# Attention with relative bias, then a max-out feed-forward: scoring the left-over queries plainly at the head of the second visit, with both AV halves in the first

## The chip, the cores and the metric

One core of one Trainium2 chip. The metric is the time of one execution on the device, in microseconds, the median of several runs. Where two kernels are compared, the ratio is the mean time of one kernel's fast runs over that of the other's fast runs of the same rounds, so it is not quite the ratio of the medians that are quoted. With one core, a run is called slow when it is over 1.5% above the fastest run of the same kernel.

In the profile lines PE is TensorE, DVE VectorE, ACT ScalarE, POOL GpSimd and SP SyncE. A line of a timeline gives the start and the length in microseconds, engine, program line, operation, what is written `<-` what is read, the shape, and how many instructions are merged (`x8`); in brackets stands the idle time of the engine just before, and what ended it. The *span* is the time from the first to the last instruction of the profiled run.

## The reference

Eight batches of eight heads, 576 positions, head size 64. Attention with a bias that depends only on the distance of query and key; its output, 4608 rows of 512, goes through a max-out layer.

```python
scores = (1/8) * q @ k.T + bias_table[bucket(|i - j|)]     # 576 x 576 per head
attn   = exp(scores - max) / sum
x      = (attn @ v), heads side by side                    # 4608 x 512
h      = maximum(maximum(x @ w1, x @ w2), x @ w3)          # 4608 x 768
out    = h @ w_out                                         # 4608 x 512
```

576 is 4 x 128 + 64. So each head has four full tiles of 128 positions and 64 left-over ones, and two heads share one set of 128 rows ("a head pair", `hp`). The bias becomes a factor exp(bias), which differs from 1 only in a band around the diagonal and is multiplied in on VectorE ("the band product").

## The kernel before

TensorE, ScalarE (exp and some copies) and VectorE (band products, quotients, maxima, copies) work on two things at a time: the attention of one head pair, and the feed-forward of the batch before, handed out in portions. A pair has two halves. Each half begins with a *visit* (scores of 256 queries against 512 keys for both heads, in two buffers of two banks), then comes one half of the *previous* pair's AV (`next_late`), then a portion of the feed-forward (`fill`), with the scores of the left-over keys (first half) or left-over queries (second half) put in between. Names are shortened here and cuts are marked.

```python
ps_s: 2 buffers of 2 PSUM banks   # scores "sc", left-over keys "sct", left-over queries "scq"
ps_a: 2 buffers of 1 bank         # AV, "a"
ps_f: 2 buffers of 1 bank         # feed-forward, "ff"

def first(fb):  ps0 = bank(); product(ps0, fb, 0); ACT: m0 = copy(ps0)         # f
def second(fb): ps1 = bank(); product(ps1, fb, 1); DVE: m  = max(ps1, m0)      # m
def third(fb):  ps2 = bank(); product(ps2, fb, 2); DVE: hT = max(ps2, m)       # g
# a portion of an ordinary half: g of block fb-1, then f and m of block fb

def left_queries(hp, qT, kT, el):          # q tail is block diagonal: 128 columns for two heads
    sc = ps_s.tile([P, KT, 2 * 64], ...)
    for t in range(KT):
        mm(sc[:, t, :], lhsT=kT[:, P * t : P * t + P], rhs=qT[:, QM : QM + P])
    exp(eq, sc)

# second half of a pair
visit(qT, kT, e4, 1)                                   # 8 matmuls, two exps
quotients = next_late()                                # AV of the previous pair, half 1
times_band(hp, e4, 1, 0, QM, inorder)                  # band product
quotients()                                            # reciprocal, product into x_sb
...
def queries():
    left_queries(hp, qT, kT, el)
    times_band(hp, e4, 3, 0, QM, inorder)
fill(rate, lambda: times_band(hp, e4, 2, 0, QM, inorder), queries)
times_band_left(hp, el)
```

TensorE's and VectorE's instructions are kept in program order. With two "ff" banks, the third product of a portion (m) takes the bank of the first (g), which is free when VectorE has done g's maximum, hT.

The softmax here doesn't subtract the row's maximum and nothing guards it: scores larger than these inputs give would overflow.

## Time and profile before

| | before |
|---|---|
| time, median of 4 runs | 325.96 us (323.77 to 326.36) |
| span of the profiled run | 324.3 us |
| one batch in the steady part (first score matmul to that of the next batch) | 33.88 us |
| one pair with an ordinary portion in both halves | 8.47 us |
| PE idle before the feed-forward matmuls | 0.0 us |
| PE wait for keys transposed by DMA (batches 2 to 7) | none |

The batch time is read off the timeline of TensorE: the first score matmul of corresponding visits stands at 164.43 and 198.31 us. The lines themselves are in the prediction.

### The profile page before, as it was taken

To read this page: it belongs to the slowest core of one execution; us is meant where nothing else is said; L and a number is where in the kernel's file an instruction comes from. 1 tells how busy PE (TensorE), PEld (TensorE's weight loads), DVE (VectorE), ACT (ScalarE), POOL (GpSimd) and SP (SyncE) were. 2 spreads that over 40 slices of the span, in tenths; PEclk is the share of its full clock that TensorE was granted. 3 is DMA by queue.
4 is the path that set the end of the run, shared out by engine and by line. 5 is a ranking of instruction groups with operands and counts; after the bars stand their busy time and mean duration, and the time that the engine had idled before them with its cause. 6 is when DMAs were issued, how large, how long until landed. Compare 5 with 4: busy or idle time off the path is not lost.

```text
span 324.3 us, 8019 instructions
## 1 busy us (share of the span) xinstructions
PE 310.4 (96%) x3232; PEld 177.1 (55%) x3232; DVE 216.0 (67%) x537; ACT 201.8 (62%) x274; POOL 112.6 (35%) x151
## 2 busy tenths in 40 slices
PE   7757999999999999999999999999999999999995
PEld 2345776787555555555555555555555554444442
DVE  6476787777666766676667766777767675454452
ACT  3947798798677667776777677667776651121221
POOL 8941977109857852194109700500000000000000
PEclk9978999999999999999999999999999999999999
DMA  9999999949999999999989998996032003301103
GB/s 163 188 207 198 154 162 153 164 109 127 192 160 155 159 181 168 118 129 164 200 81 127 175 209 76 104 205 119 1 73 98 35 3 73 132 0 65 67 0 129
DMA packets 165541, 40.72 MB, mean 126 GB/s; under 512 B 155384, under 2 KB 161024, under 8 KB 165504
## 3 DMA queue, kind: packets, MB, share of 16 engines
q0 software_dynamic: 103904, 16.66, 74.8%
q1 hardware_dynamic: 59840, 23.08, 38.7%
q10 hardware_dynamic: 1760, 0.47, 0.6%
q8 instruction: 25, 0.41, 0.5%
q14 instruction: 12, 0.10, 0.1%
HBM read 35.39 MB, written 9.45 MB: 138 GB/s over the span
## 4 chain that ended last, share of the span: by engine, by line
PE 86%; ACT 4%; POOL 3%; DMA 3%; DVE 2%; issue 1%; POOLq 0%; ACTq 0%
PE ps L94 42%; PE a L94 15%; PE pso L94 14%; PE sc L94 9%; ACT e L522 3%; PE sct L94 3%; PE scq L94 2%; DMA vt<-in_v_dram 2%; POOL q_sb L143 1%; POOL vx L143 1%; PE tp L97 1%; DMA out_dram<-osb 1%; DVE e L516 1%; ACT el L522 1%; POOL qtail L160 0%
## 5 line engine op out<-in xcount | busy, mean ns | idle before, releaser
L94 PE MATMUL ps<-xT,w_bf 128*128 128x512 bf16 (+1 forms) x720 | 156.4, 359 | 0.0
L522 ACT ACTIVATE e<-sc 128x1024 bf16<-128x1024 f32 x128 | 124.3, 1026 | 24.7 <-PE sc L94 24.1
L94 PEld LDWEIGHTS <-w_bf 128*128 128x128 bf16 x720 | 66.1, 98 | 57.1 <-issue 1.5
L516 DVE TENSOR_TENSOR e<-e,hank 128x512 bf16<-128x512 bf16 (+2 forms) x136 | 59.7, 467 | 26.9 <-ACT e L522 24.9
L337 ACT ACTIVATE m<-ps 128x512 bf16<-128x512 f32 x54 | 32.3, 598 | 66.0 <-PE ps L94 63.7
L343 DVE TENSOR_TENSOR m<-ps,m 128x512 bf16<-128x512 f32 x54 | 37.3, 690 | 45.7 <-ACT el L522 25.8
L94 PEld LDWEIGHTS <-kT 64*128 64x128 bf16 (+1 forms) x704 | 35.7, 96 | 38.6 <-issue 22.8
L94 PE MATMUL pso<-wo_bf,hT 128*128 128x512 bf16 (+2 forms) x222 | 51.0, 373 | 0.0
L94 PE MATMUL a<-vx,e 128*128 128x65 bf16 x1024 | 46.4, 195 | 0.0
L94 PE MATMUL a<-vt,el 128*128 128x130 bf16 (+1 forms) x192 | 40.3, 216 | 3.4 <-DMA vt<-in_v_dram 3.4
L143 POOL DMA_DIRECT2D vx<-in_v_dram x32 | 28.3, 892 | 43.4 <-PE a L94 38.5
L94 PE MATMUL sc<-qT,kT 64*128 64x256 bf16 x512 | 40.6, 272 | 2.4 <-DVE kT L110 1.0
L94 PEld LDWEIGHTS <-e 128*128 128x128 bf16 x1024 | 42.0, 99 | 1.0 <-issue 0.2
L348 DVE TENSOR_TENSOR hT<-ps,m 128x512 bf16<-128x512 f32 x54 | 37.0, 685 | 4.9 <-PE ps L94 3.1
L609 DVE TENSOR_TENSOR x_sb<-a,rd 128x256 bf16<-128x256 f32 (+1 forms) x64 | 31.4, 491 | 2.2
L94 PEld LDWEIGHTS <-el 128*128 128x128 bf16 x448 | 24.5, 98 | 14.8 <-issue 10.3
L94 PEld LDWEIGHTS <-hT 128*128 128x128 bf16 x222 | 20.2, 98 | 20.6 <-DVE hT L348 0.4
L110 DVE COPY osb<-pso 128x512 f32<-128x512 f32 (+1 forms) x33 | 22.7, 687 | 13.2 <-PE pso L94 9.4
L167 POOL DMA_DIRECT2D q_sb<-in_q_dram x24 | 22.2, 924 | 17.2 <-DVE x_sb L609 15.3
L522 ACT ACTIVATE el<-sct 128x640 bf16<-128x640 f32 (+2 forms) x36 | 23.2, 647 | 5.5 <-PE sct L94 4.9
L167 POOL DMA_DIRECT2D k_sb<-in_k_dram x24 | 22.0, 916 | 5.3 <-DMA vx<-in_v_dram 3.8
L522 ACT ACTIVATE el<-scq 128x512 bf16<-128x512 f32 x32 | 19.0, 595 | 6.6 <-PE scq L94 6.6
(69 smaller groups left out, 169.8 us busy)
## 6 DMA issues: line engine op xcount, KB each, us to landing
out_dram<-osb SPq DMA_DIRECT2D x35, 256.0 KB, 3.3
vx<-in_v_dram POOLq DMA_DIRECT2D x32, 128.0 KB, 6.2
q_sb<-in_q_dram POOLq DMA_DIRECT2D x26, 128.0 KB, 8.0
k_sb<-in_k_dram POOLq DMA_DIRECT2D x24, 128.0 KB, 8.9
w_bf<-in_moe_w_dram POOLq DMA_DIRECT2D x3, 768.0 KB, 13.4
xT<-in_k_dram SPq DMA_DIRECT2D x6, 128.0 KB, 4.6
hank<-w_dr SPq DMA_DIRECT2D x2, 384.0 KB, 6.2
wo_bf<-in_moe_w_out_dram POOLq DMA_DIRECT2D x1, 768.0 KB, 7.9
```

What stands on the lines that cost most here:

```text
L94: inorder(nc.tensor.matmul(*args, **kw))
L97: inorder(nc.tensor.transpose(*args))
L110: return inorder(nc.vector.tensor_copy(out_, in_))
L143: in_turn(b, nc.gpsimd.dma_start(out=dst[:, t, h0:h1, :], in_=x[:, t, h0:h1, :]))
L167: loads.append(in_turn(b, nc.gpsimd.dma_start(out=dst[:, t], in_=main_part(src, b)[:, t])))
L337: nc.scalar.activation(out=st[fb]["m0"][:], in_=ps0, func=ACTF.Copy)
L343: inorder(nc.vector.tensor_tensor(out=m[:], in0=ps1, in1=st[fb]["m0"][:], op=ALU.max))
L348: inorder(nc.vector.tensor_tensor(out=hT[:, fb * CH : fb * CH + CH], in0=ps2, in1=st[fb]["m"][:], op=ALU.max))
L516: put(nc.vector.tensor_tensor(out=e4[:, t, :, lo:hi], in0=e4[:, t, :, lo:hi], in1=hank[:, 2 * hp : 2 * hp + 2, c0:c1][:, :, ::-1], op=ALU. ...
L522: nc.scalar.activation(out=out_, in_=in_, func=ACTF.Exp, scale=inv_sqrt_d)
L609: divided[b, hp, half] = inorder(nc.vector.tensor_tensor(out=x_sb[b][:, 2 * half : 2 * half + n, P * hp : P * hp + P].rearrange("p t (h d) ...
```

## The change

The intent: the left-over queries need only 64 columns per head. Instead of a block-diagonal operand with half zeros, score each head on its own 64 rows, two heads at once, directly beside the visit's own 64-row matmuls. For that, two banks are needed at that place, and the AV banks are made free by doing both AV halves in the pair's first half. As the query tail is plain now, the left-over keys need 576 columns and not 640.

The diff is shortened.

```diff
-    def q_diag(b, par, h0, h1): ...               # two DMAs per batch
+    def load_q_tail(b):                           # one DMA, 64 partitions, 8 heads
+        dst = qtail[b % 2][0 : S - KT * P].rearrange("p g (h d) -> p (g h) d", h=2)
+        return in_turn(b, nc.gpsimd.dma_start(out=dst, in_=q[b, :, KT * P : S, :].rearrange(...)))
 ...
-    def visit(qT, kT, e4, c, mid=None):
+    def turn_left_queries(qT, kT, banks):
+        for t in range(KT):
+            for par, bank in enumerate(banks):
+                r = slice(64 * par, 64 * par + 64)
+                mm(bank[:, 64 * t : 64 * t + 64], lhsT=kT[r, P * t : P * t + P], rhs=qT[r, QM:S])
+
+    def visit(qT, kT, e4, c, mid=None, el=None):
+        if el is not None:
+            banks = [ps_a.tile([P, KT * 64], F32, tag="a", name="scq") for _ in range(2)]
+            turn_left_queries(qT, kT, banks)
+            put_left_queries(el, banks)           # one exp per bank
 ...
+        together = b > 1 and (b, hp) != (2, 0)
 ...
-        fill(rate, lambda: left_keys(hp, qT, kT, el, 0, S + 64))
+        fill(rate, *([lambda: next_late()()] if together else []),
+             lambda: left_keys(hp, qT, kT, el, 0, S))
-        visit(qT, kT, e4, 1)
+        visit(qT, kT, e4, 1, el=el if together else None)
-        quotients = next_late()
+        quotients = None if together else next_late()
         times_band(hp, e4, 1, 0, QM, inorder)
-        quotients()
+        if quotients: quotients()
 ...
         def queries():
-            left_queries(hp, qT, kT, el)
+            if not together: left_queries(hp, qT, kT, el)
```

Cut: the narrower tiles, the transposes by DMA of 64 rows ("crossbar"), one AV matmul of 130 columns in place of two of 65, and `left_queries` in the 64-row form for the nine pairs that are not "together".

More of the change, by code (lines that the diff above doesn't have):

```diff
@@ L120, in constants @@
         if i == 0:
-            inorder(nc.vector.memset(qtail[i][:], 0.0))
+            inorder(nc.vector.memset(qtail[i][64:, :, :], 0.0))
         inorder(nc.vector.memset(vt[i][:], 0.0))
@@ L147, in diag @@
         return dst[r, h0 // 2 : h1 // 2, r]
-    def q_diag(b, par, h0, h1):
-        return diag(qtail[b % 2], par, h0, h1)
+    def load_q_tail(b):
+        dst = qtail[b % 2][0 : S - KT * P].rearrange("p g (h d) -> p (g h) d", h=2)
+        return in_turn(b, nc.gpsimd.dma_start(out=dst, in_=q[b, :, KT * P : S, :].rearrange("h p d -> p h d")))
     def k_diag(b, par, h0, h1):
@@ L167, in load_qk @@
                 loads.append(in_turn(b, nc.gpsimd.dma_start(out=dst[:, t], in_=main_part(src, b)[:, t])))
-        for src, dst in ((q, q_diag), (k, k_diag)):
-            for par in range(2):
-                load = nc.gpsimd.dma_start(out=dst(b, par, 0, H), in_=tail_part(src, b, 0, H, par))
-                loads.append(in_turn(b, load))
+        loads.append(load_q_tail(b))
+        for par in range(2):
+            load = nc.gpsimd.dma_start(out=k_diag(b, par, 0, H), in_=tail_part(k, b, 0, H, par))
+            loads.append(in_turn(b, load))
         if behind:
@@ L243 @@
     constants(0)
-    inorder(nc.vector.memset(qtail[1][:], 0.0))
+    inorder(nc.vector.memset(qtail[1][64:, :, :], 0.0))
     dve_copy(pick[:], ids[:])
@@ L261 @@
     load_main(q, 0, 0, H, batch[0][0], 2, KT)
-    load_tail(q, 0, 0, H, q_diag)
+    load_q_tail(0)
     load_v(0, 0, H)
@@ L299, in load_hank @@
         ))
-    bandt = const.tile([P, HP, 2 * P], BF16, name="bandt")
+    bandt = const.tile([P, HP, 192], BF16, name="bandt")
     def make_bandt():
@@ L308, in make_bandt @@
             c = BAND // 2 - 64 * par
-            for c0, c1 in ((192, 256), (0, 192)):
-                dve_copy(bandt[r, :, c0:c1], hank[r, par::2, c : c + c1 - c0][:, :, ::-1])
+            dve_copy(bandt[r, :, :], hank[r, par::2, c : c + 192][:, :, ::-1])
     def ffn(t0, nt, last):
@@ L443, in one @@
         def one(j, t):
+            n = P if t < KT or j else S - KT * P
             src = batch[b][j][:, t].rearrange("p h d -> p (h d)") if t < KT else (
-                (qtail, ktail)[j][b % 2][:].rearrange("p h c -> p (h c)")
+                (qtail, ktail)[j][b % 2][0:n].rearrange("p h c -> p (h c)")
             )
-            inorder(nc.sync.dma_start_transpose(out=made[j][:, :, P * t : P * t + P], in_=src))
+            inorder(nc.sync.dma_start_transpose(out=made[j][:, :, P * t : P * t + n], in_=src))
         for t in range(KT + 1):
@@ L454, in qk_tiles @@
     def qk_tiles():
-        return [qkt.tile([P, HP, (KT + 1) * P], BF16, tag=n, name=n) for n in ("qT", "kT")]
+        return [qkt.tile([P, HP, n], BF16, tag=x, name=x) for x, n in (("qT", S), ("kT", (KT + 1) * P))]
     def first_transposes(hp):
@@ L487, in more_transposes @@
         tr(tp[:, QS : QS + P], qtail[0][:, hp, :], ident[:])
-        dve_copy(qk[0][0][:, hp, QS:], tp[:, 0 : QS + P])
+        dve_copy(qk[0][0][:, hp, QS:], tp[:, 0 : S - QS])
     def second_transposes(made, hp):
@@ L505, in second_transposes @@
         tail = [
-            copy(made[j][:, hp, KT * P :], tp[:, j, KT * P : (KT + 1) * P])
-            for j, copy in enumerate((dve_copy, act_copy))
+            copy(made[j][:, hp, KT * P :], tp[:, j, KT * P : n])
+            for j, (copy, n) in enumerate(((dve_copy, S), (act_copy, (KT + 1) * P)))
         ]
@@ L522, in exp, with put_left_queries @@
         nc.scalar.activation(out=out_, in_=in_, func=ACTF.Exp, scale=inv_sqrt_d)
-    def visit(qT, kT, e4, c, mid=None):
+    def put_left_queries(el, banks):
+        eq = el[:, S:].rearrange("p (t h q) -> p t h q", t=KT, h=2)
+        for par, bank in enumerate(banks):
+            exp(eq[:, :, par, :], bank.rearrange("p (t q) -> p t q", t=KT))
+    def turn_left_queries(qT, kT, banks):
+        for t in range(KT):
+            for par, bank in enumerate(banks):
+                r = slice(64 * par, 64 * par + 64)
[5 more added lines that the diff above has]
+            put_left_queries(el, banks)
         for tt in range(0, KT, 2):
@@ L552, in times_bandt @@
         inorder(nc.vector.tensor_tensor(
-            out=el[:, S - 192 : S + 64], in0=el[:, S - 192 : S + 64], in1=bandt[:, hp, :], op=ALU.mult
+            out=el[:, S - 192 : S], in0=el[:, S - 192 : S], in1=bandt[:, hp, :], op=ALU.mult
         ))
     def left_queries(hp, qT, kT, el):
-        sc = ps_s.tile([P, KT, 2 * 64], F32, tag="sc", name="scq")
-        for t in range(KT):
-            mm(sc[:, t, :], lhsT=kT[:, P * t : P * t + P], rhs=qT[:, QM : QM + P])
-        eq = el[:, S + 64 :].rearrange("p (t h q) -> p t h q", t=KT, h=2)
-        exp(eq, sc[:].rearrange("p t (h q) -> p t h q", h=2))
+        sc = ps_s.tile([P, 2, CH], F32, tag="sc", name="scq")
+        turn_left_queries(qT, kT, [sc[:, par, 0 : KT * 64] for par in range(2)])
+        eq = el[:, S:].rearrange("p (t h q) -> p h t q", t=KT, h=2)
+        exp(eq, sc[:, :, 0 : KT * 64].rearrange("p h (t q) -> p h t q", t=KT))
     def times_band_left(hp, el):
-        last_tile = el[:, S + P * KT - 64 :].rearrange("p (h q) -> p h q", h=2)
+        last_tile = el[:, S + P * KT - P :].rearrange("p (h q) -> p h q", h=2)
         inorder(nc.vector.tensor_tensor(
@@ L593, in attend @@
         if half:
+            mm(
+                x[:, 4:6, :], lhsT=el[:, S - P : S], rhs=vl[:, hp, :, 0:AW],
+                start=True, stop=False, skip_group_check=True,
+            )
             for par in range(2):
-                mm(
-                    x[:, 4 + par, :], lhsT=el[:, S - P + 64 * par :][:, 0:P], rhs=vl[:, hp, par, 0:AW],
-                    start=True, stop=False, skip_group_check=True,
-                )
                 for kt in range(KT):
                     mm(
-                        x[:, 4 + par, :], lhsT=el[:, S + P * kt + 64 * par :][:, 0:P],
+                        x[:, 4 + par, :], lhsT=el[:, S - 64 + P * kt + 64 * par :][:, 0:P],
                         rhs=v[:, kt, 2 * hp + par, 0:AW],
@@ L643, in e_tiles @@
             ep.tile([P, KT, 2, QM], BF16, tag="e4", name="e4"),
-            ep.tile([P, S + 64 + KT * P], BF16, tag="el", name="el"),
+            ep.tile([P, S + KT * P], BF16, tag="el", name="el"),
         )
@@ L669, in load_second @@
             if h0 == 0:
-                load_tail(q, 1, 0, H, q_diag)
+                load_q_tail(1)
                 load_tail(k, 1, 0, H, k_diag)
@@ L734, in keys @@
         def keys():
-            left_keys(hp, qT, kT, el, QS, S + 64)
+            left_keys(hp, qT, kT, el, QS, S)
         def queries():
@@ L794 @@
             spread_packed(hp + 1, nc.vector)
-        fill(rate, lambda: left_keys(hp, qT, kT, el, 0, S + 64))
+        fill(
+            rate, *([lambda: next_late()()] if together else []),
+            lambda: left_keys(hp, qT, kT, el, 0, S),
+        )
         times_bandt(hp, el)
-        visit(qT, kT, e4, 1)
+        visit(qT, kT, e4, 1, el=el if together else None)
         store_outputs()
@@ L805 @@
             turned.pop(0)()
-        quotients = next_late()
+        quotients = None if together else next_late()
         times_band(hp, e4, 1, 0, QM, inorder)
-        quotients()
+        if quotients:
+            quotients()
         if b == 1 and hp + 1 < HP:
@@ L822, in queries @@
         def queries():
-            left_queries(hp, qT, kT, el)
+            if not together:
+                left_queries(hp, qT, kT, el)
             times_band(hp, e4, 3, 0, QM, inorder)
```

## The prediction

> **What bounds the kernel now.** I read the page's busy shares and the chain of work that ended last, then a table of stretches, then the timeline of one steady head pair engine by engine, and the groups of instructions for durations.
>
> ```profile
> PE 310.4 (96%) x3232; PEld 177.1 (55%) x3232; DVE 216.0 (67%) x537; ACT 201.8 (62%) x274; POOL 112.6 (35%) x151
> ...
> PE 86%; ACT 4%; POOL 3%; DMA 3%; DVE 2%; issue 1%; POOLq 0%; ACTq 0%
> ```
>
> TensorE is busy 96% of the span and holds 86% of the chain. A busy PE is not proof of a bound (ends are modelled), so I look for holes. The stretches (start:end, length, then busy time of PE, PEld, DVE, ACT, POOL) are full from 60 us on:
>
> ```profile
> 130.00:160.00 30.00, 30.00 (x319) 16.26 (x317) 20.47 (x49) 21.03 (x28) 14.27 (x18) 1.00 1.70 153
> 160.00:190.00 30.00, 30.00 (x333) 16.75 (x334) 21.30 (x50) 20.73 (x27) 14.27 (x18) 1.00 1.53 142
> ```
>
> VectorE and ScalarE are busy only 70%. One batch (4 head pairs) repeats every 33.88 us, and a pair with the ordinary feed-forward portions lasts 8.47 us (first big matmul of the second half at 153.05, 161.52, 169.99). Second half of such a pair, on PE, ACT and DVE (start, length, instruction):
>
> ```profile
> 160.06 0.61 PE L94 MATMUL sc<-qT,kT 64*128 64x256 bf16 x8
> 160.61 0.23 PE L94 MATMUL a<-vt,el 128*128 128x130 bf16 x1
> ...
> 161.52 1.89 PE L94 MATMUL ps<-xT,w_bf 128*128 128x512 bf16 x8
> 163.24 0.39 PE L94 MATMUL scq<-qT,kT 128*128 128x128 bf16 x4
> 163.47 1.03 PE L94 MATMUL ps<-xT,w_bf 128*128 128x512 bf16 x4
> 164.43 0.61 PE L94 MATMUL sc<-qT,kT 64*128 64x256 bf16 x8
> ```
> ```profile
> 160.50 1.94 ACT L522 ACTIVATE e<-sc 128x1024 bf16<-128x1024 f32 x2 [0.27 <-PE sc L94]
> 163.44 0.60 ACT L337 ACTIVATE m<-ps 128x512 bf16<-128x512 f32 x1 [1.01 <-PE ps L94]
> 163.94 0.59 ACT L522 ACTIVATE el<-scq 128x512 bf16<-128x512 f32 x1
> ```
> ```profile
> 161.55 0.56 DVE L516 TENSOR_TENSOR e<-e,hank 128x768 bf16<-128x768 bf16 x1 [0.43 <-ACT e L522]
> 162.03 0.19 DVE L608 RECIPROCAL rd<-a 128x6 f32<-128x6 f32 x1
> 162.25 0.56 DVE L609 TENSOR_TENSOR x_sb<-a,rd 128x384 bf16<-128x384 f32 x1
> 162.73 0.68 DVE L348 TENSOR_TENSOR hT<-ps,m 128x512 bf16<-128x512 f32 x1
> ```
>
> Start-to-start times add up without a hole: visit 0.55, AV of the second half 0.91 (160.61 to 161.52), eight big matmuls 1.72, left queries 0.23, four big ones plus the return to 64-row matmuls 0.96; sum 4.37, and 164.43 - 160.06 = 4.37. So the steady part is bound by PE. But this fit is tight. The feed-forward has two PSUM banks ("ff"). The portion here is third product g, first f, second m; m takes g's bank, which VectorE's hT instruction frees. hT ends at 163.41; m begins at 163.47. The chain visit, exp, band product, quotients, hT has no slack: it is just covered by AV, g, f and left queries. This is where I expect the change to bite.
>
> **What the Trainium skill says.** (1) "TensorE: Matmul & The Clock Gate", Back-to-back issue gap: N/2.4 + 2.5 ns when warm. The trace agrees: the four 128-column left-query matmuls take 0.225 us (163.24 to 163.47), eight 512-column ones 1.72, i.e. 215 ns each. (2) The same page, Part 3: matmuls and weight loads on different row groups run at once. Agrees: eight 64-row, 256-column matmuls fit in 0.55 us, where one after the other takes 8 x 109 = 0.87. (3) "TensorEngine Tiling (Array Packing)", Key Properties: changing the tiling mode drains the engine. Agrees: from the end of the big matmuls' issue (163.47 + 0.86 = 164.33) to the first 64-row matmul is 0.10 us, and the eight take 0.55 instead of 4 x 109 = 0.44, so about 0.1 on each side. (4) "ScalarE: Activation LUTs", What ACT_TABLE_LOAD costs: an ACTIVATE with immediates takes 186 + 0.833 N ns and neighbours overlap by about 93. The trace has 1026 ns for 1024 columns, 595 for 512 and 410 for 256, and 0.50 us from the 512-wide m to the next start, an overlap of 0.10.
>
> **The change, part by part**, for the 23 "together" pairs (batch 2 from its second pair, batches 3 to 7).
>
> Left queries. Removed: 4 full-row matmuls of 128 columns, 0.225 us. Added: 8 of 64 columns, in row pairs, directly before the visit's own 64-row matmuls, so no further mode change. Estimate from (1) and (2): 4 x 29 ns, with the start some 0.13 us. Saves 0.10 on PE. On ScalarE one 512-column exp becomes two of 256: from 0.50 to 2 x 0.31 us (410 less 0.10), and, more important, they move ahead of the visit's exps.
> Left keys. 576 instead of 640 columns: 64/2.4 = 27 ns of PE, 53 ns of ScalarE.
> AV. Two 65-column matmuls become one of 130: nothing in columns, nothing saved (65 columns take 29.5 ns each, 130 take 57). The move matters: 0.91 us of PE work and 0.70 us of VectorE work (reciprocal and product, 162.03 to 162.73) go from the second half to the first.
> So the pure PE account is -0.13 us a pair, 23 x 0.13 = -3.0 us.
>
> First half after: 64-row visit, AV 0, g, AV 1, f, left keys, m. About 4.97 us long (4.10 - 0.03 + 0.91). More cover for hT, hence no wait. AV 1's quotients end near 3.9 us after its start; the left queries need that bank at 4.97: no wait.
>
> Second half after, from the first left-query matmul as 0. PE: left queries 0.13, visit to 0.68, g to 1.54, f to 2.40, and m wants to start at 2.40: AV and the old left queries (1.14 us) no longer stand before it. The chain for its bank: last left-query matmul ends near 0.29; exp one starts 0.33, exp two 0.64, the visit's first exp 0.95 (it was 0.44), ends 1.97; band product starts 2.00; hT 0.48 later at 2.48 (no quotients between), ends 3.16; m can start at 3.21. PE stands still for 0.81 us. The half lasts 3.21 + 0.86 + 0.09 = 4.16 us. Pair: 4.97 + 4.16 = 9.13 against 8.47, +0.67.
>
> Which halves have g, f, m? From the PE timeline, the portions rotate over eight halves of a batch: second halves of pairs 0, 2 and 3 have it; that of pair 1 is two output groups, whose banks are free (no stall), and the early g with the output after it falls in a first half, now with more cover. Batches 3 to 7 give 15, batch 2 gives 2: 17 stalls. 17 x 0.81 = +13.8; less 3.0: +10.8.
>
> The rest. In the other nine pairs the left queries become 64-row matmuls among full-row ones: 0.13 + 2 x 0.09 against 0.225, less 0.03: about +0.06 each, +0.5. At the start one DMA issue of 0.64 us fewer ahead of the V tail, for which PE waits 3.4 us there: up to -0.6, if issue and not transfer decides. These cancel. The fewer POOL issues and crossbar rows later are off the path.
> Sum: 326.1 + 10.8 = about 337 us.
>
> **The rivals.**
> A, PE stays the bound: the stall is covered somewhere, and 3 us are saved, 323 us. For it: 100% PE and 30% idle in VectorE and ScalarE. Against: hT ends 0.06 us before its use already, and the change takes 1.14 us of cover and puts 0.5 us of exps into the chain.
> B, the stall is half as long: the scheduler puts the visit's exp ahead of the left queries' exps. Then hT ends at 0.13 + 1.49 + 0.48 + 0.68 = 2.78 and m waits 0.4: 17 x 0.4 - 3 = +4, 330 us. Against: the left-query scores are ready first and come first in the program; ScalarE now runs in program order.
> C, the left queries wait for the AV banks' quotients at each pair's second half. It would add on all 23 pairs: at 0.3 us each, +7 on top, 344. Against: 1 us of slack in my working.
> D, eight weight loads, not the columns, set the left queries' pace: 8 x 29 ns = 0.24, the saving of 0.10 is gone, +2.3, 339. Against: 64-row loads already overlap in the visit.
>
> **Range and chances.** The centre is the sum; B, with a shorter stall, gives the low end, 330; C or D or longer exps give the high end, 343. Faster by over 2% (below 319.6) needs more than the whole PE saving: 3%. Within 2% (to 332.6) is A or B: 20%. Slower: 77%.
>
> **What would show it.** Right: PE idle before ps of about 13 us, put down to DVE hT, against 0.0 now; in a steady second half no AV matmuls, and m 0.8 us after f's issue ends; batch period about 33.9 + 3 x 0.81 - 0.5 = 35.8; two 256-wide exps before each visit pair, and the band product 2.0 us after the first left-query matmul; PE busy time itself smaller by the matmuls removed. Wrong: PE without holes and a period below 33.9 (A), or the idle time before scq, released by x_sb (C), or left-query blocks longer than 0.2 us (D). The weakest step is the order of instructions on ScalarE and VectorE, which I take from the program.

## The result

The change measures 339.82 us median (335.62 to 344.07, four runs, two of them slow) against 325.96. The ratio of the fast runs is 1.0347, 95% interval 1.0247 to 1.0447: slower, and inside the predicted range of 330 to 343. The profiled run is a fast one, span 336.2 us.

The page of the kernel after: busy time, the chain that ended last by engine, and the line of the large feed-forward matmuls (busy, mean ns, then PE's idle time before them and who ended it).

```profile
PE 308.2 (92%) x3287; PEld 172.1 (51%) x3328; DVE 214.5 (64%) x535; ACT 199.6 (59%) x297; POOL 108.1 (32%) x143
...
PE 60%; ACT 13%; DMA 9%; DVE 7%; issue 4%; POOL 4%; SPq 3%; POOLq 0%; ACTq 0%
...
L94 PE MATMUL ps<-xT,w_bf 128*128 128x512 bf16 (+1 forms) x694 | 155.0, 360 | 12.4 <-DVE hT L348 9.9
```

PE is 2 us less busy in a span that is 12 us longer. The feed-forward matmuls, which had 0.0 us of idle time before them, now have 12.4, of which VectorE's hT ended 9.9. Two more waits stand in the list of PE's waits (total, times, longest):

```profile
PE ps L94 <- DVE hT L348: 9.9, 17, 0.6
PE sc L94 <- DMA kT<-k_sb: 3.5, 1, 3.5
```

17 times is the number of halves that the prediction counted. The same stretches of the steady part as before show PE no longer full:

```profile
130.00:160.00 30.00, 28.35 (x311) 15.23 (x315) 19.15 (x45) 19.85 (x31) 14.21 (x18) 1.00 1.86 141
160.00:190.00 30.00, 27.88 (x315) 15.11 (x319) 20.61 (x49) 19.91 (x30) 13.12 (x16) 1.00 1.49 120
```

And a second half of an ordinary pair, on PE, ACT and DVE:

```profile
167.24 0.29 PE L94 MATMUL scq<-qT,kT 64*128 64x64 bf16 x8
167.37 0.60 PE L94 MATMUL sc<-qT,kT 64*128 64x256 bf16 x8
167.90 1.90 PE L94 MATMUL ps<-xT,w_bf 128*128 128x512 bf16 x8
170.38 1.02 PE L94 MATMUL ps<-xT,w_bf 128*128 128x512 bf16 x4 [0.58 <-DVE hT L348]
171.34 0.61 PE L94 MATMUL sc<-qT,kT 64*128 64x256 bf16 x8
```
```profile
167.56 0.66 ACT L523 ACTIVATE el<-scq 128x256 bf16<-128x256 f32 x2 [0.19 <-PE scq L94]
168.11 1.95 ACT L523 ACTIVATE e<-sc 128x1024 bf16<-128x1024 f32 x2
```
```profile
169.17 0.56 DVE L517 TENSOR_TENSOR e<-e,hank 128x768 bf16<-128x768 bf16 x1 [0.90 <-ACT e L523]
169.65 0.68 DVE L348 TENSOR_TENSOR hT<-ps,m 128x512 bf16<-128x512 f32 x1
170.25 0.88 DVE L517 TENSOR_TENSOR e<-e,hank 128x768 bf16<-128x768 bf16 x2
```

The eight big matmuls from 167.90 end their issue at 167.90 + 1.73 = 169.63. The next group starts at 170.38, 0.05 us after hT has ended at 170.33. So PE loses 0.75 us from start to start; the wait list says 0.58 because it counts from the modelled end of the last matmul. hT had to follow the band product (169.17), that the visit's first exp (168.11), and that the two left-query exps (167.56). The left queries themselves are as cheap as hoped: 167.24 to 167.37, 0.13 us.

Where the 12.0 us between the two spans lie, by the first score matmul of each batch:

| | before | after | gained (+) or lost by after |
|---|---|---|---|
| batch 2 begins | 66.89 | 63.45 | +3.44 |
| batch 2 lasts | 29.77 | 36.75 | -6.98 |
| batches 3 to 6, each | 33.88 | 35.57 | 4 x -1.69 |
| batch 7 and the rest | 92.07 | 93.75 | -1.68 |

The steady part is as predicted. The second row is not: the kernel after begins batch 2 sooner and then waits 3.5 us for its keys.

### The profile page after: what moved, and what is told of

Same layout as the page of the kernel before. It is cut to its first block, busy times and chain, and to the rows that moved or that the text cites. A ratio compares the mean times of both kernels' runs of the same rounds, so it can differ in the third digit from the quotient of the medians.

```text
span 336.2 us, 8192 instructions
## 1 busy us (share of the span) xinstructions
PE 308.2 (92%) x3287; PEld 172.1 (51%) x3328; DVE 214.5 (64%) x535; ACT 199.6 (59%) x297; POOL 108.1 (32%) x143
## 4 chain that ended last, share of the span: by engine, by line
PE 60%; ACT 13%; DMA 9%; DVE 7%; issue 4%; POOL 4%; SPq 3%; POOLq 0%; ACTq 0%
PE ps L94 28%; PE a L94 12%; PE pso L94 12%; ACT e L523 6%; PE sc L94 5%; DMA xT<-in_q_dram 5%; DVE hT L348 4%; DVE m L343 3%; ACT el L523 3%; DMA kT<-k_sb 3%; ACT m L337 3%; SPq L448 3%; POOL q_sb L143 1%; POOL vx L143 1%; PE sct L94 1%
## 5 line engine op out<-in xcount | busy, mean ns | idle before, releaser
L94 PE MATMUL ps<-xT,w_bf 128*128 128x512 bf16 (+1 forms) x694 | 155.0, 360 | 12.4 <-DVE hT L348 9.9
L94 PEld LDWEIGHTS <-w_bf 128*128 128x128 bf16 x720 | 64.7, 98 | 74.1 <-issue 20.0
L94 PEld LDWEIGHTS <-kT 64*128 64x128 bf16 (+1 forms) x832 | 29.9, 95 | 39.3 <-issue 24.7
L94 PE MATMUL pso<-wo_bf,hT 128*128 128x512 bf16 (+2 forms) x207 | 47.5, 373 | 0.9 <-issue 0.2
L94 PE MATMUL sc<-qT,kT 64*128 64x256 bf16 x512 | 41.7, 276 | 6.2 <-DMA kT<-k_sb 3.5
L94 PE MATMUL a<-vx,e 128*128 128x65 bf16 x1024 | 44.7, 193 | 0.0
L94 PEld LDWEIGHTS <-e 128*128 128x128 bf16 x1024 | 40.6, 97 | 2.9
L94 PE MATMUL a<-vt,el 128*128 128x130 bf16 x160 | 35.6, 222 | 0.8 <-DMA vt<-in_v_dram 0.8
L523 ACT ACTIVATE el<-scq 128x256 bf16<-128x256 f32 (+1 forms) x55 | 20.5, 416 | 9.9 <-PE scq L94 9.7
L523 ACT ACTIVATE el<-sct 128x576 bf16<-128x576 f32 (+2 forms) x36 | 21.4, 598 | 8.1 <-PE sct L94 8.0
```

The lines of the kernel that those rows point to most:

```text
L94: inorder(nc.tensor.matmul(*args, **kw))
L523: nc.scalar.activation(out=out_, in_=in_, func=ACTF.Exp, scale=inv_sqrt_d)
```

## The experiments

All kernels below gave correct results. "Batch" is the steady batch time; "keys" is the sum of PE's waits for transposed keys of batches 2 to 4; "rest" is the span less that of the kernel before less 5.75 x (batch - 33.88), that is, what the steady part does not explain (23 pairs are 5.75 batches). The time is the median of all runs; the four columns on the right are of one profiled run. "hT wait" is as the wait list has it, which counts from the modelled end of a matmul and so misses waits below about 0.17 us. The runs came in jobs: e1, e2, e3 and e5 on chip 9, then e4 and e6 to e8 on chip 1, e9 to e11 on chip 0, e12 on chip 9; each has its own runs of the kernel before (medians 325.3 to 326.9).

| kernel | time us | ratio, 95% interval | batch us | hT wait us | keys us | rest us |
|---|---|---|---|---|---|---|
| before | 325.96 | 1 | 33.88 | 0 | 0 | 0 |
| after | 339.82 | 1.0347 (1.0247 to 1.0447) | 35.57 | 9.9 | 3.5 | 2.2 |
| e1_plain_only | 330.39 | 1.0151 (1.008 to 1.0222) | 34.19 | 0 | 3.9 | 1.5 |
| e2_av_moved | 334.5 | 1.0254 (1.0151 to 1.0357) | 34.46 | 0 | 5.0 | 4.2 |
| e3_av_split | 334.22 | 1.0275 (1.02 to 1.035) | about 35.3 | 5.0 | 2.8 | 0.6 |
| e4_exps_behind | 335.05 | 1.0279 (1.021 to 1.0348) | 34.60 | 4.4 | 2.5 | 1.6 |
| e5_band_behind | 332.69 | 1.0195 (1.012 to 1.027) | 33.58 | 0 | 7.0 | 8.9 |
| e6_v2_later | 330.16 | 1.0162 (1.0112 to 1.0212) | 33.57 | 0 | 3.2 | 2.3 |
| e7_diagonal | 324.98 | 0.998 (0.9936 to 1.0025) | 33.69 | 0 | 0 | -0.7 |
| e8_diagonal_v2_later | 326.29 | 1.0037 (0.9992 to 1.0081) | 33.69 | 0 | 3.0 | 3.4 |
| e9_split_start | 331.95 | 1.0146 (1.006 to 1.0233) | 33.58 | 0 | 6.7 | 8.2 |
| e10_split_late | 323.12 | 0.9905 (0.9854 to 0.9957) | 33.57 | 0 | 0 | -2.2 |
| e11_split_all | 328.27 | 1.0031 (0.9941 to 1.0121) | 33.58 | 0 | 4.5 | 5.4 |
| e12_again (e10 once more) | 327.35 | 1.0045 (1.0003 to 1.0086) | 33.57 | 0 | 3.6 | 4.4 |

### The four parts of the chain

**e1_plain_only**: the plain forms alone.

```diff
-        together = b > 1 and (b, hp) != (2, 0)
+        together = False
```

> The plain left-over queries and 576 key columns alone, at the old place in the program; AV one half in each visit as before. Theory (the stall is the chain visit, exp, band product, hT, bank of m, which only the moves of AV and of the left-query exps break): no wait of ps for hT, batch period 33.9 + 4 x 0.06 = 34.1 us, time 326 + 1 to 2 = 327 to 328 us. Rival (the time comes from the loads and transposes of the plain tails, which the kernel after also shows as a 3.5 us wait of the scores for transposed keys of batch 2): the wait for the keys remains and the time stays at or above 333 us.

The wait for hT is gone and the batch lasts 34.19 us, 0.08 a pair above the kernel before: the 64-row left queries among full-row matmuls take 0.22 us (174.17 to 174.39) after a change of mode of 0.09, and not the 0.13 that they take just before the visit. So the moves, not the plain forms, make the stall. But the time is 330.39, 2 to 3 us above the expectation, and 3.9 us of waits for keys are there. The rival was right about a part.

**e2_av_moved**: both AV in the first half, left queries at the old place.

```diff
-        visit(qT, kT, e4, 1, el=el if together else None)
+        visit(qT, kT, e4, 1)
-            if not together:
-                left_queries(hp, qT, kT, el)
+            left_queries(hp, qT, kT, el)
```

> Both AV in the first half as in the change, but the left queries stay where they were (score bank, before the last product), in the 64-row form. Theory: no exps in the chain, no quotients either; hT ends 1.49 + 0.48 + 0.68 = 2.65 us after the visit begins, m is due at 0.55 + 1.73 + 0.31 = 2.58, so a wait of about 0.1 us in 17 halves; batch period about 34.4, time about 330 us. Rival (the loss is the lost cover of AV alone, whatever the exps do): 0.6 us in each of 17 halves as in the change, 337 us or more.

The batch of 34.46 us is 0.27 above e1, 0.09 for each of its three ordinary second halves: the expected 0.1. (The wait list shows none; but in one such half hT ends at 177.88 and m begins at 177.93, 0.32 us after the start of the left queries before it, against 0.22 in e1.) The loss of the AV's cover alone is nearly harmless, because the quotients leave VectorE's chain together with it. The time, 334.5, is 4 us over the expectation, again by waits for keys (5.0 us).

**e3_av_split**: left queries at the head of the visit, AV one half in each.

```diff
-        fill(rate, *([lambda: next_late()()] if together else []), lambda: left_keys(...))
+        fill(rate, lambda: left_keys(...))
-        quotients = None if together else next_late()
+        quotients = next_late()
```

> The left queries at the head of the second visit in the AV banks as in the change, but AV again one half in each visit, so the second half's AV takes a bank that the left-query exps free. Theory: exps in the chain and quotients too; the visit's first exp ends at 1.91 us, band 1.93, hT 3.11 to 3.79, m at 3.84; m is due at 3.43 (AV waits 0.1 for its bank): wait 0.4 us in 17 halves and 0.1 in all; time about 326 + 7 - 3 + 2 = 332 us. Rival (the loss is AV in the first half alone): no wait for hT, 325 us.

PE's first wait:

```profile
PE ps L94 <- DVE hT L348: 5.0, 17, 0.3
```

Half of the stall is there although AV has its old cover: 0.3 us by the wait list, which is 0.46 from start to start in one half (176.88 to 177.34), where 0.4 was expected. AV waits a further 0.1 for its bank, as expected. The time, 334.22, is 2 us over the expectation, of which the waits for keys are 2.8. So the exps at the head do more harm than the move of AV, and the two together do the most.

**e4_exps_behind**: as the change, but ScalarE takes the left-query exps after the visit's two exps; TensorE's order is the same.

```diff
             turn_left_queries(qT, kT, banks)
-            put_left_queries(el, banks)
         for tt in range(0, KT, 2):
             ...
-            exp(e4[...], sc[:])
+            inorder(exp(e4[...], sc[:]))        # in the second visit
+        put_left_queries(el, banks)             # exps kept in this order
```

> The change, with ScalarE made to take the two left-query exps behind the visit's two exps (TensorE's order is unchanged). Theory: the visit's first exp starts 0.57 us after the first left-query matmul instead of 0.87, so the band product and hT come 0.3 earlier: the wait of ps for hT goes from 0.75 to 0.4 us start to start (0.58 to 0.25 as the wait list counts it), 17 times; batch period 35.57 - 3 x 0.33 = 34.6, time 337 - 6 = 331 us, with 2 us either way from the waits for keys in batches 2 and 3. Rival (the exps are not in the chain): period stays 35.6, time 337.

```profile
PE ps L94 <- DVE hT L348: 4.4, 17, 0.3
```

Batch 34.60 us, as expected. Putting two exps of together 0.55 us behind instead of ahead gives back (35.57 - 34.60) / 3 = 0.32 us per stall. This is the world of the prediction's rival B, and the stall, 0.43 us from start to start, is as long as B said. The time is not: 335.05 us where 331, give or take 2, was expected (B: 330). The profiled run, 331.83, is the fastest of the four, so its trace does not show where the others lost time.

**e5_band_behind**: as the change, but the first band product of the second half goes behind hT on VectorE.

```diff
-        times_band(hp, e4, 1, 0, QM, inorder)
+        if not together: times_band(hp, e4, 1, 0, QM, inorder)
 ...
-        fill(rate, lambda: times_band(hp, e4, 2, 0, QM, inorder), queries)
+        fill(rate, *([lambda: times_band(hp, e4, 1, 0, QM, inorder)] if together else []),
+             lambda: times_band(hp, e4, 2, 0, QM, inorder), queries)
```

> The change with one move: in the second half the first band product goes behind the hT product on VectorE, so hT no longer waits for any exp of the visit. Theory: hT starts when g ends (1.71 us after the first left-query matmul), ends 2.43, m is due at 2.40: the wait falls from 0.75 start to start to under 0.1 us in 17 halves, batch period to about 33.5, time to 338 - 17 x 0.7 = 326 us, perhaps 324. Rival (m waits for something else than the band product ahead of hT, or the time is in the transposes): the time stays within 2 us of the change, 336 to 340.

A second half of it on PE and on DVE:

```profile
194.38 0.29 PE L94 MATMUL scq<-qT,kT 64*128 64x64 bf16 x8
194.50 0.60 PE L94 MATMUL sc<-qT,kT 64*128 64x256 bf16 x8
195.04 2.20 PE L94 MATMUL ps<-xT,w_bf 128*128 128x512 bf16 x9
```
```profile
196.11 0.69 DVE L348 TENSOR_TENSOR hT<-ps,m 128x512 bf16<-128x512 f32 x1 [0.70 <-PE ps L94]
196.72 0.55 DVE L517 TENSOR_TENSOR e<-e,hank 128x768 bf16<-128x768 bf16 x1
```

hT now waits for its product and for nothing else. The ninth big matmul, which is m's first, starts 0.30 us after the eighth (196.56 to 196.86), where 0.22 is the usual distance: of the 0.75 us, 0.08 is left, too short for the wait list. The batch takes 33.58 us, less than the 33.88 of the kernel before: here the change's own saving is seen, 0.30 us a batch. So the link "band product ahead of hT" carried nearly the whole stall. Yet the time is 332.69 us and not 326. The reason is in PE's waits and in the stretch from 60 to 80 us of the kernel before, of the kernel after and of this one (the number after the POOL entry is the granted clock):

```profile
PE sc L94 <- DMA kT<-k_sb: 7.0, 3, 3.8
```
```profile
60.00:80.00 20.00, 20.00 (x299) 15.19 (x297) 15.51 (x40) 17.32 (x23) 6.80 (x8) 1.00 1.16 123
```
```profile
60.00:80.00 20.00, 16.29 (x242) 12.23 (x241) 11.55 (x30) 12.43 (x19) 4.89 (x6) 0.91 1.04 114
```
```profile
60.00:80.00 20.00, 15.42 (x214) 11.38 (x212) 9.96 (x28) 11.54 (x15) 2.47 (x3) 0.83 1.08 110
```

TensorE waits for the keys of batch 2, and after the wait it is granted half its clock for 3.4 us (6.8 in e5_band_behind). Half clock for 3.4 us loses about 1.7 us of work, an estimate; it fits the pair in which it falls in the kernel after, which takes 11.4 us against 6.0, of which 3.55 is the wait. So the keys have their own account, and the remaining runs asked for its cause.

### Where the waits for keys come from

**e6_v2_later**: e5 with V of batch 2 asked for one pair later (`hp == (3, 1, 0)[...]` for `(2, 1, 0)[...]`).

> The kernel with the band product behind hT, and V of batch 2 asked for one pair later. Open is why that kernel waits 7 us in all for transposed keys in batches 2 and 3 and so gains nothing on the kernel before. Theory A: TensorE reaches batch 2 some 3 us earlier than before, and the transposes of batch 2's keys share the queues with V of batch 2; without V the keys land earlier, the waits at 65 to 70 us fall from 4.6 to under 1.5, no half clock follows, time 326 to 328. Theory B (the plain tails made the loads slower): no change within 2 us, 331 to 333; or V itself comes late and is waited for.

Half of it came: the waits in batch 2 fell to 0.8 us, but 2.4 us of waiting and a half clock came in batch 3, and the time is 330.16 us.

**e7_diagonal**: the kernel before, with the order of e5 and left queries scored on 64 rows from the diagonal blocks; tails, loads, key columns and AV of the left rows as before.

```diff
+                    mm(bank[:, 64 * t : 64 * t + 64], lhsT=kT[r, P * t : P * t + P],
+                       rhs=qT[r, QM + 64 * par : QM + 64 * par + 64])
```

> The kernel before with its block-diagonal tails, their loads, 640 key columns and the old AV of the left rows; new are only the order (both AV in the first half, band product behind hT) and the left queries scored on 64 rows from the diagonal blocks at the head of the second visit. Both theories of the main stall: no wait for hT, batch period 33.88 - 0.40 = 33.5 us. Theory B (plain tails slow the loads): no waits for keys, time about 324. Theory A (the order of loads is too late for a TensorE that is ahead): the start is that of the kernel before, so no lead and only small waits in batch 2, but waits of 1 to 2 us from batch 3 on as soon as TensorE gains on the loads; 325 to 328.

**e8_diagonal_v2_later**: e7 with the move of e6.

> The same with V of batch 2 asked for one pair later. Theory A: waits for keys below 1 us, 323 to 325 us. Theory B: as without the move, within 1 us.

e7 has no wait for keys, a batch of 33.69 us (33.5 was expected) and the time of the kernel before (0.998). That spoke for theory B. But e8, with the same block-diagonal tails, has 3.0 us of such waits, and the later V, which was to help, seems to help e6 and to harm e8. Neither theory accounts for both.

**e9_split_start, e10_split_late, e11_split_all**: e5 with the plain query tail loaded by two DMAs of four heads, for batches 0 and 1, for batches 2 to 7, or for all.

```diff
+        if b < 2:      # e9;  b > 1 in e10;  always in e11
+            return [in_turn(b, nc.gpsimd.dma_start(out=dst[:, h : h + 4], in_=src[:, h : h + 4])) for h in (0, 4)]
```

> The kernel with plain tails and the band product behind hT (332.7 us, 5 to 7 us of it waits for keys in batches 2 and 3); the plain query tails of batches 0 and 1 are loaded with two DMAs of four heads each instead of one of eight, so the start issues as many DMAs as the kernel before. Theory A (a head start of TensorE by some 2 to 3 us, won by the DMA that is gone at the start, runs into keys that land no earlier): batch 2 is reached at about 66 us as in the kernel before, the wait there falls below 1 us, time 326 to 328. Theory B (the later plain tails slow the loads of each batch): waits as before, 331 to 333.

> The same kernel, now with only the tails of batches 2 to 7 in two DMAs and the start as in the change. Theory A: no change, 331 to 333 us, first waits at 65 to 70 us. Theory B in the form that one DMA of eight heads is worse than two of four: the waits in batch 3 go, 326 to 329.

> All tails in two DMAs. Theory A: as with the split at the start alone, 326 to 328 us. Theory B in that form: waits gone, 325 to 327. If all three stay at 331 to 333 us with waits for keys, it is neither the head start nor the number of DMAs, and the plain form itself (64 partitions, one transposed tail of 64 rows) is left.

In e9 the waits are the same as in e5. It is not the clean test of theory A that it was meant to be, since it reaches batch 2 at 64.46 us and not at the expected 66; but its keys land at 69.3, so that even the kernel before, which gets there at 66.89, would have waited. So theory A falls in its simple form. e10 has no waits, 323.12 us, and is the only version whose interval lies below 1 (within 2%). But e11, which has that same split, is back at 328.27 us, and its profiled run, a slow one, has a 4.2 us wait in batch 2. The effects do not add up, so I ran e10 again.

**e12_again**: the same program as e10, in a later job on another chip.

> The kernel with band product behind hT and the tails of batches 2 to 7 in two DMAs once more, unchanged, on another allocation of a chip, with five rounds. The three split kernels did not add up: split at the start 332, late 323, both 328 us. If the 323 us belong to this program (its order and placement of transfers), it repeats: 322 to 324, ratio 0.985 to 0.995, no wait for keys, batch period 33.57. If it was the luck of a chip or an hour, the waits for keys of batches 2 and 3 come back and the time is 328 to 333 us.

```profile
PE sc L94 <- DMA kT<-k_sb: 3.4, 2, 2.9
```

It did not repeat: 327.35 us over six runs (326.12 to 328.74), against 322.11 to 323.57 over four runs in the first job, with the steady batch the same 33.57 us. In the profiled runs, 6.6 us apart, the difference is in the waits for keys (3.6 us) and the half clock after them (6.8 us long, about 3.4 us of work, an estimate). So the 323 us were the luck of that job or chip, and the waits of a single run do not rank these kernels. No version was shown to beat the kernel before; e7_diagonal equals it.

## Why the prediction was right

**The bound and the tight place.** Right. PE was full, hT ended 0.06 us before its use, and the stall came at exactly that place, in 17 halves.

**The chain.** Right in every link. e4 takes the exps out of it (0.32 us less per stall), e5 the band product (0.08 us of the stall left), e2 and e3 show the move of AV alone worth 0.09 us and the exps at the head alone worth 0.46. The stall itself was set at 0.81 us and measured 0.75: the two exps follow each other after 0.275 us (167.56 to 168.11 for both) where I took 0.31.

**The savings.** Left queries 0.13 us in place of 0.225, left keys 0.24 in place of 0.27: as worked out. The steady batch of the kernel after bears out the 0.13 a pair: 35.57 - 33.88 - 3 x 0.75 = -0.56 us, or 0.14 a pair. e5's batch shows only 0.30, or 0.08 a pair, because 0.08 us of each of its three stalls is left.

**Both AV in the first half.** Right: no wait for the AV banks appears anywhere in the list (rival C), and the left queries are not paced by weight loads (rival D).

**"These cancel".** This step of the sum failed. It set the gain at the start (one DMA fewer) against +0.5 us for the other nine pairs. In the profiled run the kernel after reached batch 2 3.4 us sooner, more than the 0.6 foreseen, and then lost more than that again: 3.55 us of waiting for keys, and the half clock after it. Together about +2 us in place of 0. The stalls came out about 1 us cheaper than predicted (17 x 0.06), so that the sum, 337 us, stands beside a mean of the fast runs of 336.8: the agreement to a fraction of a microsecond is partly two errors that cancel, the ratio of 1.035 is not. Most of the 3.4 us at the start is the wait for the V tail, 0.8 us in place of 3.4; how far the missing DMA made it is not shown, since e7 and e8, which start like the kernel before, have 3.2 and 1.3 us of it. With one DMA for the plain tail batch 2 begins at 63.4 to 63.9 us in all nine traces, with two (e9, e11) at 64.5 and 64.6, with the block-diagonal tails at 66.9, 65.6 and 64.7.

**Two slips in the working.** The pair's +0.67 is 9.13 - 8.47 = 0.66, and rival C, at 344 us, lies outside the range whose high end it was to give. Neither touches the argument.

**What stays open.** Why the keys of batches 2 and 3 land late in some programs and jobs. The traces settle a part. The last full tile of batch 2's keys is asked for at 57.4 us in the kernel before and at 57.2 in the kernel after, but lands after 7.6 us (at 65.0) in the one and after 10.3 us (at 67.5) in the other. From the critical chain of the kernel after:

```profile
57.20 10.26 DMA kT<-k_sb
```

So of the 3.55 us of waiting about 2.5 come from the later landing and 1 from TensorE's earlier arrival, an estimate from these times. The form of the tails does not decide alone: with plain tails these keys land at 65.1 us or before in e1, e6, e10 and e12, with block-diagonal ones at 67.4 in e8. Nor does the arrival: e10 and e12, one program, both reach batch 2 at 63.87 us, and only e12 waits (0.7 us there, 2.9 in batch 3). What delays the transfers was not settled by these runs.

## What to carry to other kernels

When an engine is 100% busy and others are 70% busy, the work of the bound engine can be what covers a chain through the others, as here; before moving such work, add up the chain from the visit to the release of the next bank and compare it with what is left in front. An instruction that is cheap for its engine (two exps of 256 columns) can cost time by standing ahead of a longer one that somebody waits for (0.32 us in each stall here), though its engine has time to spare; where order is free, put first what frees a bank, as hT before the band product did. And measure the steady part and the start apart: here up to 8.9 us of 330 (e5) came from outside the steady part, and a gain of 1% in one job was gone in the next.

## What the Trainium skill lacked or had wrong

- "TensorE: Matmul & The Clock Gate", Part 1, the table of states, gives half clock after an idle window of about 3.4 us. In e3_av_split a single wait of 2.00 us, TensorE being busy before and after it, was followed by a granted clock of 0.91 in the stretch from 60 to 80 us, which is half clock for about 3.5 us (0.51 from 67.0 to 70.5 us). Single waits of 2.1 us (e4) and 2.4 us (e6) did the same, one of 1.6 us (e2, batch 3) did not. So a wait of 2 us can be enough. The two lines:

```profile
66.09 0.28 PE L94 MATMUL sc<-qT,kT 64*128 64x256 bf16 x2 [2.00 <-DMA kT<-k_sb]
```
```profile
60.00:80.00 20.00, 17.97 (x255) 12.89 (x253) 12.40 (x32) 14.23 (x20) 6.29 (x8) 0.91 1.21 119
```

- The same page, Part 2, Back-to-back issue gap, says that in a stream of weight loads and matmuls 128 columns take about 81 ns and 512 about 131. Here each matmul has its own weight load, and 128 columns take 56 ns, 512 take 215 and 65 take 29.5: the formula that the page gives for the isolated case holds, with the loads hidden.
- "TensorEngine Tiling (Array Packing)", Key Properties, says that a change of mode drains the engine and gives no figure. Here it is about 0.1 us on each side, and with it 64-row left queries among full-row matmuls save nothing: e1_plain_only's batch is 0.31 us longer than before.
- None of the pages read says how much the landing of the same transfers differs between jobs. e10_split_late and e12_again are one program on two chips: 0 and 3.6 us of waits, 323 and 327 us.
